# Inverse FFT tables through TensorE and PSUM in place of transposing DMA, other instructions for the last chunk's tiles, and a newly searched order, in a kernel of two sequence layers

## The chip, the cores and the metric

The kernel runs on one core of one Trainium2 chip. The metric is the device time of one execution in microseconds (us). Most executions of a kernel agree within 0.3%; the profile is one execution taken by the hardware profiler. A single core's runs are called fast unless they lie over 1.5% above the fastest of the same kernel; one execution of all told here was not fast, and it is kept out of the comparisons. Engines are written as in the profile: PE is TensorE's matmuls, PEld its weight loads, DVE is VectorE, ACT is ScalarE, POOL is GpSimd, SP issues most DMAs. Ratios are the mean time of one kernel's fast runs over the mean time of the other's fast runs of the same rounds, so they are not quite the ratio of the medians that stand beside them.

## The reference

Two layers, each applied twice, A, B, A, B, on a sequence of 2048 positions with 640 channels, in bf16:

```python
# A: a diagonal complex state-space layer
h = Lam_bar * h + Bu[:, t, :]                    # recurrence over t
y = 2.0 * einsum(hseq, Cmat).real + x * Dskip
# B: a short shift filter, a long convolution by FFT of length 4096, a gate
kv = k_shift * v
y = irfft(rfft(kv, padded) * rfft(ssm_k, padded))[:2048] + kv * ssm_D
return q * y
# the whole
x = x + A(layernorm(x)); x = x + B(layernorm(x))
x = x + A(layernorm(x)); x = x + B(layernorm(x))
```

Layer B's factor (all of it but the gate by the normalized x) does not depend on x, so the kernel computes it once, in its first 200 us, and stores it to DRAM as `ysd`. The FFT is done as matmuls with tables of cosines and sines. The result is compared with the reference within a tolerance.

## The kernel before

Some 860 small tasks are ordered by a table of priorities, `WHEN`, which was found by a search and is part of the source. A list scheduler turns it into one fixed order per engine and the instructions are emitted in that order:

```python
WHEN = {"warm": -5, "yt_io0": 2.55, ..., "yt_Ci": 21.14, "yt_Si": 22.8, "yt_nsi": 30.27, ...}   # cut
...
order.sort(key=lambda t: (t.start, t.idx))
for t in order:
    t.emit(t.eng)
```

So each engine has a fixed order; what an instruction waits for is decided at run time. All matmuls share four PSUM buffers of 128 x 1024 float32. A task that copies a product out of PSUM may go to ACT or to DVE, as the table decides:

```python
def evac(nc, eng, out, in_):
    if eng == "act":
        nc.scalar.activation(out, in_, ACT.Copy)
    else:
        nc.vector.tensor_copy(out, in_)
```

The tables `Ci` and `Si` of the inverse FFT are the transposes of the forward tables `Cf` and `Sf` (17 blocks of 128 columns each), and `NSi` is the negated `Si`:

```python
for a, b in (("Ci", "Cf"), ("Si", "Sf")):
    def e_tr(_, a=a, b=b):
        nc.sync.dma_start_transpose(out=T[a].get()[:], in_=T[b].get().rearrange("p q k -> p (q k)"))
    ...
def e_nsi(_):
    nc.vector.tensor_scalar(T["NSi"].get(), T["Si"].get(), -1.0, None, ALU.mult)
```

Second, another table on DVE, `a_t0`, which is used only some 90 us after it is made; it is not part of the change, but the argument comes back to it:

```python
def e_t0(_):                      # task "a_t0", two instructions of 1290 float32 columns
    v.tensor_scalar(r, y, MAGIC, None, ALU.add)
    v.scalar_tensor_tensor(r, r, MAGIC, y, ALU.subtract, ALU.subtract)
```

The end of layer B's second use. The last chunk of 512 positions is finished tile by tile (128 positions each) by two scalar_tensor_tensor instructions (STT) on DVE; results are stored in pairs of tiles:

```python
# abridged: index expressions are shortened
if len(qs) == 1:     # the last chunk: each tile by itself
    nc.vector.scalar_tensor_tensor(bu(), s_x[q], nmean, s_Y[q], ALU.add, ALU.mult)
    nc.vector.scalar_tensor_tensor(s_Y[q], bu(), rstd, s_x[q], ALU.mult, ALU.add)
...
if out is not None and q % 2 == 1:      # store two tiles, 320 KB
    nc.sync.dma_start(out=out[...2 tiles...], in_=s_Y[:, 2 * t:2 * t + 2, :])
```

## Time and profile before

| what | before |
|---|---|
| device time, median of 3 runs (lowest, highest) | 358.5 us (357.69, 358.55) |
| span of the profiled execution, mean granted TensorE clock | 356.8 us, 0.987 |
| TensorE's last matmul ends | 345.70 us |
| last read of PSUM by DVE starts | 345.89 us |
| last sum on DVE ends | 353.60 us |

The table is read as a relay. Up to 345.70 us TensorE sets the pace: it is busy nearly without a break from 140 us on. From 345.89 to 353.60 us, DVE alone finishes the last tiles. From 353.60 to 356.8 us the last store is under way. A change of the head (the first 140 us) shows as a shift of 345.70; a change of the tail shows in the two distances after it. The page itself is shown in the prediction.

### The profile page before, as it was taken

What the parts mean: (1) busy time and instruction counts of PE and PEld (TensorE: products, weight loads), DVE (VectorE), ACT (ScalarE), POOL (GpSimd) and SP (SyncE); (2) the same over time, 40 slices, a digit from 0 to 9 for tenths busy, and PEclk for the clock granted to TensorE, in tenths of its full rate; (3) what the DMA queues carried; (4) which work ended last, traced back from release to release, by engine and by line L of the source; (5) the groups of instructions that cost most, each with busy time, mean ns of one, the idle gap of its engine ahead of it and who ended that gap; (6) DMA issues with size and microseconds to landing.
All of it is one profiled execution on the core that took longest, in us unless ns stands there. A gap on an engine that the chain in (4) does not pass through costs nothing.

```text
span 356.8 us, 8409 instructions
## 1 busy us (share of the span) xinstructions
PE 327.5 (92%) x3534; PEld 247.6 (69%) x3565; DVE 315.1 (88%) x479; ACT 256.4 (72%) x406; POOL 20.8 (6%) x51
## 2 busy tenths in 40 slices
PE   7686998989998997999999999999999999999970
PEld 7346876867686986986685677686866767755640
DVE  8799798798799797999999969979999679999896
ACT  3999798898799999943378599797256577306850
POOL 5841003000000000000000000000000000000000
PEclk9999899999999999999999999999999999999996
DMA  7999999999999982790226690605032022220141
GB/s 193 208 235 188 182 184 217 193 186 202 237 245 163 184 174 46 144 233 2 62 73 119 137 333 34 147 18 132 0 68 81 3 16 59 75 75 2 50 172 73
DMA packets 118712, 45.91 MB, mean 129 GB/s; under 512 B 111629, under 2 KB 112914, under 8 KB 118674
## 3 DMA queue, kind: packets, MB, share of 16 engines
q1 hardware_dynamic: 118528, 45.36, 59.9%
q8 instruction: 28, 0.46, 0.5%
q14 instruction: 10, 0.08, 0.1%
q10 hardware_dynamic: 146, 0.01, 0.0%
HBM read 17.38 MB, written 7.86 MB: 71 GB/s over the span
## 4 chain that ended last, share of the span: by engine, by line
PE 69%; ACT 10%; DVE 8%; DMA 7%; issue 3%; SPq 2%; DVEq 0%; ACTq 0%
PE ps L859 31%; PE ps L770 11%; PE ps L773 11%; ACT b L382 6%; PE ps L608 3%; PE ps L1163 3%; DMA b<-in_A_C_im_dram 2%; DMA b<-in_B_v_dram 2%; DVE b L1169 2%; PE ps L1313 2%; DMA b<-b 2%; PE ps L1314 1%; PE ps L1208 1%; SPq L536 1%; DMA b<-in_B_k_dram 1%
## 5 line engine op out<-in xcount | busy, mean ns | idle before, releaser
L382 ACT ACTIVATE b<-ps 128x1024 bf16<-128x1024 f32 (+3 forms) x125 | 109.6, 945 | 29.5 <-PE ps L773 25.5
L859 PEld LDWEIGHTS <-b 128*128 128x128 bf16 x880 | 67.7, 98 | 48.3
L859 PE MATMUL ps<-W,b 128*128 128x128 bf16 (+1 forms) x629 | 95.7, 298 | 0.6
L770 PE MATMUL ps<-b,BT 128*128 128x256 bf16 x400 | 56.8, 273 | 0.0
L773 PE MATMUL ps<-b,BT 128*128 128x256 bf16 x400 | 56.7, 273 | 0.0
L808 DVE TENSOR_TENSOR_SCAN b<-rtab,b 128x1290 bf16<-128x1290 f32 x16 | 44.7, 2833 | 0.3
L773 PEld LDWEIGHTS <-BT 128*128 128x128 bf16 x400 | 39.1, 98 | 4.5
L770 PEld LDWEIGHTS <-BT 128*128 128x128 bf16 x400 | 38.6, 98 | 4.4
L726 ACT ACTIVATE b<-b,nmr,rstd 128x640 bf16<-128x640 f32 (+1 forms) x43 | 37.0, 915 | 6.2 <-DVE nmr L693 6.2
L681 ACT ACTIVATE junk<-b,nmean 128x640 bf16<-128x640 f32 x48 | 39.7, 828 | 1.5
L1232 PE MATMUL ps<-b,b 128*128 128x128 bf16 x170 | 35.1, 219 | 1.2 <-ACT G L382 0.7
L1235 PE MATMUL ps<-b,b 128*128 128x128 bf16 x170 | 35.4, 219 | 0.0
L1237 PE MATMUL ps<-b,b 128*128 128x128 bf16 x150 | 32.8, 219 | 0.0
L1234 PE MATMUL ps<-b,b 128*128 128x128 bf16 x150 | 32.8, 219 | 0.0
L384 DVE CAST b<-ps 128x1024 bf16<-128x1024 f32 (+2 forms) x24 | 26.2, 1109 | 6.3 <-PE ps L1208 2.7
L867 ACT ACTIVATE b<-ps 128x640 f32<-128x640 f32 x16 | 11.1, 697 | 22.8 <-PE ps L859 22.8
L859 PE MATMUL ps<-G,b 128*128 128x128 bf16 (+1 forms) x152 | 26.5, 295 | 0.4
L1163 PE MATMUL ps<-b,fd 128*128 128x512 bf16 x73 | 18.6, 380 | 3.8 <-POOL fd L1141 2.0
L1313 PE MATMUL ps<-b,b 128*128 128x128 bf16 x160 | 19.4, 219 | 2.6 <-ACT b L382 2.1
L1314 PE MATMUL ps<-b,b 128*128 128x128 bf16 x160 | 19.2, 219 | 0.0
L552 ACT ACTIVATE b<-b,s_F 128x640 f32<-128x640 bf16 x20 | 17.2, 859 | 1.8 <-DVE W L556 1.4
L556 DVE SCALAR_TENSOR_TENSOR W<-b,s_F 128x640 bf16<-128x640 bf16 x20 | 17.4, 882 | 1.0 <-ACT b L552 0.7
(210 smaller groups left out, 560.3 us busy)
## 6 DMA issues: line engine op xcount, KB each, us to landing
b<-in_A_x_dram SPq DMA_DIRECT2D x8, 640.0 KB, 4.9
b<-ysd SPq DMA_DIRECT2D x8, 640.0 KB, 5.1
b<-in_B_ssm_k_dram SPq DMA_DIRECT2D x5, 512.0 KB, 8.6
kvd<-b SPq DMA_DIRECT2D x5, 512.0 KB, 4.3
b<-kvd SPq DMA_DIRECT2D x5, 512.0 KB, 5.4
ysd<-b SPq DMA_DIRECT2D x5, 512.0 KB, 5.0
out_dram<-b SPq DMA_DIRECT2D x8, 320.0 KB, 2.2
tab<-in_A_B_re_dram SPq DMA_DIRECT2D x1, 800.0 KB, 7.4
```

What stands on the lines that cost most here:

```text
L382: nc.scalar.activation(out, in_, ACT.Copy)
L681: nc.scalar.activation(small.junk, src(q), ACT.Square, bias=st["nmean"][:, i:i + 1], scale=1.0, accum_out=st["ssq"][:, i:i + 1])
L726: nc.scalar.activation(dst, src, ACT.Identity, bias=st["nmr"][:, i:i + 1], scale=st["rstd"][:, i:i + 1])
L770: nc.tensor.matmul(pb[:, jj, c2, :], lhsT=aw["BT1"][:, c2, j, k, :], rhs=uT[:, 0:2, k, :], start=(k == 0), stop=False)
L773: nc.tensor.matmul(pb[:, jj, c2, :], lhsT=aw["BT0"][:, c2, k, j * P:(j + 1) * P], rhs=uT[:, 2:4, k, :], start=False, stop=(k == NJ - 1))
L808: nc.vector.tensor_tensor_scan(gv, rt, gv, 0.0, ALU.mult, ALU.add)
L859: nc.tensor.matmul(pc[:, o0:o1], lhsT=lh, rhs=rh, start=(n == 0), stop=(n == len(ops) - 1))
L1163: nc.tensor.matmul(pk[:, 512 * b:512 * (b + 1)], lhsT=s_ds.get()[:, l, :], rhs=kT[:, t0:t0 + 512], start=(l == 0), stop=(l == 3))
L1232: nc.tensor.matmul(ps[:, g, 0, :], lhsT=T["Cf"].get()[:, q, :], rhs=are, start=True, stop=single)
L1234: nc.tensor.matmul(ps[:, g, 0, :], lhsT=T["Sf"].get()[:, q, :], rhs=A[:, 2 * q + 1, :], start=False, stop=True)
L1235: nc.tensor.matmul(ps[:, g, 1, :], lhsT=T["NSf"].get()[:, q, :], rhs=are, start=True, stop=single)
L1237: nc.tensor.matmul(ps[:, g, 1, :], lhsT=T["Cf"].get()[:, q, :], rhs=A[:, 2 * q + 1, :], start=False, stop=True)
```

## The change

It has three parts and a consequence. (1) `Ci` and `Si` come from 34 TensorE transposes (the data block as weights, the identity as moving operand) into PSUM and six copies out of it, so the SP queue loses two transposing DMAs. (2) Tiles 0 to 2 of the last chunk get a normalization (ACT or DVE), a bf16 product and a sum in place of the two STTs; the sums of the last two chunks may go to GpSimd. (3) The last chunk's tiles are stored one by one. The consequence: the whole table `WHEN` was searched again, and nearly every one of its keys has a new value.

```diff
 # (1)
-        nc.sync.dma_start_transpose(out=T[a].get()[:], in_=T[b].get().rearrange("p q k -> p (q k)"))
+    for q0, q1 in ((0, 6), (6, 12), (12, NQ)):
+        for q in range(q0, q1):
+            nc.tensor.matmul(s_ps.get()[:, (q - q0) * P:(q - q0 + 1) * P], lhsT=T[b].get()[:, q, :], rhs=consts["ident_bf"][:], start=True, stop=True)
+        ...
+        evac(nc, eng, T[a].get()[:, q0:q1, :].rearrange("p q k -> p (q k)"), s_ps.get()[:, 0:(q1 - q0) * P])   # eng: ACT or DVE
 # (2)
-            if len(qs) == 1:
+            if qs[0] == 3:                      # only tile 3 keeps its two STTs
...
-                            nc.vector.tensor_tensor(s_Y.get()[:, q, :], b, x, ALU.add)
+                            (nc.gpsimd if eng == "pool" else nc.vector).tensor_tensor(s_Y.get()[:, q, :], b, x, ALU.add)
+                    engs, ests = (("dve", "pool"), (0.77, 1.4)) if out is not None and c >= NCH - 2 else ...
 # (3)
-        if out is not None and q % 2 == 1:      # 320 KB
+        if len(groups) > 1:                     # the last chunk: 160 KB each
+                nc.sync.dma_start(out=out[...][:, q & 1], in_=s_Y.get()[:, q, :])
 # and the table
-    "warm": -5, "yt_io0": 2.55, ..., "a_t0": 26.17, ...        (862 keys)
+    "warm": 0.28, "yt_io0": 0.89, ..., "a_t0": 29.65, ...      (877 keys)
```

## The prediction

> **What bounds the kernel now.** I read the page from the top (busy shares, slices), then the busy time by stretch of the span, then the end of the chain of waits and the DVE timeline of the last 15 us, and last the queue of SP and the GpSimd rows, because the change touches those.
>
> The first view says that no engine is far from full, and that the weight lies unevenly.
>
> ```profile
> PE 327.5 (92%) x3534; PEld 247.6 (69%) x3565; DVE 315.1 (88%) x479; ACT 256.4 (72%) x406; POOL 20.8 (6%) x51
> ...
> PE   7686998989998997999999999999999999999970
> DVE  8799798798799797999999969979999679999896
> ```
>
> The second view cuts the span in three: head, middle and tail (us from the start; then busy us and instructions of each engine, the clock, the DMA share).
>
> ```profile
> 0.00:140.00 140.00, 122.95 (x1701) 99.54 (x1713) 118.54 (x222) 124.47 (x164) 20.77 (x51) 0.99 1.02 193
> 140.00:341.00 201.00, 199.90 (x1799) 145.32 (x1817) 184.19 (x236) 128.91 (x236) 0.00 (x0) 1.00 0.35 86
> 341.00:357.00 16.00, 4.70 (x42) 2.76 (x39) 12.33 (x23) 3.03 (x9) 0.00 (x0) 0.81 0.25 100
> ```
>
> In the middle TensorE is busy 199.90 of 201 us: it is the bound there, and it can only end earlier if it starts that stretch earlier or has less to do. In the head it idles 140 - 122.95 = 17 us; ACT (124 of 140 us) and the DMA share (1.02) are the full ones. In the tail TensorE is done and DVE is what ends the kernel. The chain of waits, cut to its end, says the same:
>
> ```profile
> 337.82 3.82 PE ps L859 x28
> 341.64 0.02 issue
> 341.66 0.83 DVE b L871 x2
> ...
> 345.89 0.82 DVE b L871 x2
> 346.72 0.81 DVE b L901
> 347.52 0.03 issue
> 347.55 0.89 DVE b L905
> 348.43 2.40 DVE b L901 x3
> 350.83 0.02 issue
> 350.86 1.68 DVE b L905 x2
> ```
>
> L871 takes the last TensorE product out of PSUM at 345.89; after it come four multiplications (L901) and four additions (L905) of the last chunk, one per tile, all on DVE; the last one starts at 352.72 and ends at 353.60. The output store that follows lands 2.2 us after its issue, and the span closes at 356.8. The measured time is 358.5, 1.7 us more than the span.
>
> **What the Trainium skill says.** First, "SBUF — State Buffer", section "Who interferes with whom": a DVE instruction with two SBUF inputs contends with a GpSimd instruction that reads SBUF, and the later one blocks. The trace agrees. GpSimd's small products (L1141) take
>
> ```profile
> L1141 POOL TENSOR_TENSOR fd<-ident_bf,skf x20: 392/394/2311, 12.5 to 55.7; 128x128 bf16<-128x128 bf16 x20
> ```
>
> 394 ns as a rule (minimum, median, maximum) and once 2311 ns, when DVE ran a two-input product (L487) that itself took 2311 ns. Second, "GPSIMD Engine Reference", section "3.1 Elementwise — side-by-side cycle accounting": about 2.6 cycles per element for a two-input operation. At the skill's 1.2 GHz that is 277 ns for 128 elements, so the 394 ns hold some 117 ns of fixed cost, and a 640-element addition comes to an estimated 1.39 + 0.12 = 1.5 us. No run shows one yet. Third, "DMA: Bandwidth & Descriptors", section "Anatomy of one DMA — SWDGE (gpsimd) path": about 2 us of a transfer are fixed. It is written for another queue, but the 320 KB stores here land after 2.2 us, so halving a store can save only a few tenths. Fourth, "TensorE: Matmul & The Clock Gate", section "Part 4: PE-mode transpose": about 390 ns alone and 275 ns in a kernel. The trace shows something cheaper for the form used here (data as weights, identity as moving operand, L572): five of them in 0.44 us, and 128-column matmuls of a stream start 0.055 us apart. The measured pitch counts.
>
> **The change, part by part.**
>
> (1) The inverse tables. Two transposing DMAs (L987) leave the SP queue; they held it 2.42 and 3.75 us, at 19.9 and 23.1 us. So 6.2 us go from a queue that is nearly always occupied in the first 60 us, and later loads can be issued up to 6 us earlier. In return: 2 tables x 17 blocks = 34 TensorE matmuls, 34 x 0.055 = 1.9 us, and 6 PSUM copies of 768, 768 and 640 columns. The rows give 0.82 us for 768 columns and 0.70 for 640 on ACT, 0.82 for 640 on DVE, thus some 4 x 0.85 + 2 x 0.76 = 4.9 us over ACT and DVE. TensorE's 1.9 us fit into its 17 us of idle time. The copies fall on ACT and DVE when ACT is busy 9.94 of 10 us (20 to 30 us). And the tables are first used near 50 us, while they are ready by about 28 us: nothing waits for them now; only the queue does. Relief and added load are of one size: up to 6 us less in the queue against some 2.5 us more on each of ACT and DVE. The order table was searched again for the new mix, so I take a little as gained: TensorE's end 0.3 us earlier, with 2 us of doubt either way.
>
> (2) Last chunk, tile by tile. Before: 8 two-input STT at 0.82 to 0.84 us pitch, 6.6 us of DVE. After: tile 3 keeps its two (1.66 us). Tiles 0 to 2 get a normalization (on ACT, 0.91 us, or on DVE, 0.56 us pitch), a bf16 product of 640 elements and a sum. L916 does 2560 in 1.49 us; with 0.16 us fixed, 640 take 0.33 + 0.16 = 0.49, or 0.42 at pitch. The sum (as L924) is 0.76 us at pitch. ACT is nearly empty in the tail (3.03 of 16 us), so I expect two of the three normalizations there: DVE has 1.66 + 0.56 + 3 x 0.42 + 3 x 0.76 = 5.8 us. That is 0.8 us less.
>
> (3) Sums shared with GpSimd, in the last two chunks: seven sums may move. GpSimd gets one only where DVE is taken for over 0.3 us in the schedule; I guess two of chunk 2 and one of chunk 3. DVE loses 3 x 0.76 = 2.3 us. But nearly everything DVE does there has two SBUF inputs (products, sums, STT), so by the skill's rule and the 2311 ns case the two engines largely take turns: three sums of 1.5 us on GpSimd can block up to 4.5 us of DVE. Only the PSUM reads (L871, 0.82 us each), normalizations and small operations go beside them. I charge 2.0 us, so this part brings 0.3 us.
>
> (4) Stores one by one: 160 KB after the last sum in place of 320 KB. Against 2 us fixed this saves perhaps 0.4 us. More stores are issued (four in place of two), hidden but for the last.
>
> There is a floor: the last tile's own chain after L871 ends at 346.71: mean 0.25, squares 1.0, root 0.4, reciprocal and product 0.4, normalization 0.6 to 0.95, product 0.45, sum 0.76, so 350.6 to 350.9 against 353.60. Parts 2 and 3 can thus bring 3 us at the most; I take 0.8 + 0.3 = 1.1. Sum: 0.3 + 1.1 + 0.4 = 1.8 us; 358.5 - 1.8 = 356.7 us.
>
> **The rivals.** One: the queue is the head's real bound, and the 6.2 us come through. For it: DMA share 1.02, and loads wait behind one another. Against it: few TensorE waits in the head name a DMA (the largest is 1.1 us); most name ACT, DVE or GpSimd. If half came through: 353.5 us. Two: ACT and DVE bound the head, and the six copies delay it by their 2.5 us with no relief: TensorE starts its full stretch later, and the tail's gain is used up: about 359 us. Three: GpSimd and DVE lock each other in the tail, so that a 1.5 us sum stands before the last tile's chain: it replaces DVE's serial work with a new wait, tail gain zero or negative, 357.5 to 358.5. Four: no contention in the tail and the chain at its floor: 3 + 0.4 us, so 355.
>
> **Range and chances.** The rivals span 353.5 to 359; I set 353.5 to 359.3 for 8 in 10 around 356.7. Over 2% faster means below 351.3, which needs both rival one and rival four in full: 0.05. Over 2% slower means above 365.7, more than all the copies added serially: 0.02. Within 2%: 0.93.
>
> **What would show it.** In the changed profile: TensorE's last matmul within 2 us of 345.7 (step 1); its idle time in the first 140 us near 17 us, with 34 new matmuls and six copies of some 0.8 us between 15 and 35 us; from the last L871 to the last sum 5.5 to 6.2 us in place of 7.7 (parts 2 and 3); GpSimd sums of 1.5 us or more, and DVE products or sums beside them stretched beyond 0.5 and 0.8 us (contention; if none is stretched, rival four); the last store landing about 0.4 us sooner. I am wrong if TensorE ends more than 3 us earlier, or if GpSimd sums stretch the last tile's chain past 353.6.

## The result, and the profile after

The changed kernel takes 358.68 us (median of 4 runs, 358.41 to 359.07); the kernel before, in the same rounds, 358.38 us (357.69 to 358.55). The ratio is 1.0013, 95% interval 0.9996 to 1.003: the same within the noise. It was forecast 1.8 us shorter.

First the engines and slices of the changed kernel.

```profile
PE 332.9 (93%) x3599; PEld 249.6 (70%) x3599; DVE 317.3 (89%) x481; ACT 260.1 (73%) x410; POOL 25.7 (7%) x54
...
PE   8889799999998998999999999999999999999980
DVE  8889999795898996999999957599999989899996
```

Nothing stands out: 34 more weight loads (3599 against 3565), five more us on GpSimd. (The page before holds 3534 of its 3565 matmuls, so PE's busy times cannot be compared to the last us.) Next the three stretches, for which the columns are as in the prediction.

```profile
0.00:140.00 140.00, 126.69 (x1735) 101.17 (x1736) 121.83 (x227) 124.93 (x164) 20.72 (x51) 0.99 0.91 185
140.00:341.00 201.00, 199.93 (x1814) 144.84 (x1814) 182.70 (x233) 128.19 (x232) 0.00 (x0) 1.00 0.33 84
341.00:358.00 17.00, 6.26 (x52) 3.62 (x49) 12.78 (x23) 6.94 (x16) 5.01 (x3) 0.82 0.34 118
```

The middle is as full as before. In the head the DMA share fell from 1.02 to 0.91: the queue was relieved, as intended. Loads also land sooner; the row of the 512 KB loads of `ssm_k` (issue to landing, last column) of the kernel before and of the changed one:

```profile
b<-in_B_ssm_k_dram SPq DMA_DIRECT2D x5, 512.0 KB, 8.6
```

```profile
b<-in_B_ssm_k_dram SPq DMA_DIRECT2D x5, 512.0 KB, 4.9
```

Yet TensorE did not end sooner. The last matmul row of the kernel before (start, duration):

```profile
344.98 0.72 PE L859 MATMUL ps<-W,b 128*128 128x128 bf16 x10
```

And the tail of the changed kernel, in order of time, from its last matmul row on:

```profile
346.54 0.72 PE L862 MATMUL ps<-W,b 128*128 128x128 bf16 x10
347.38 0.82 DVE L874 SCALAR_TENSOR_TENSOR b<-ps,b 128x640 f32<-128x640 f32 x1
...
348.45 0.90 DVE L926 TENSOR_TENSOR b<-b,b 128x640 bf16<-128x640 bf16 x2 [0.25 <-ACT b L729]
349.02 1.58 POOL L934 TENSOR_TENSOR b<-b,b 128x640 bf16<-128x640 bf16 x1 [2.51 <-DVE b L926]
349.38 1.91 DVE L934 TENSOR_TENSOR b<-b,b 128x640 bf16<-128x640 bf16 x1
...
351.47 0.88 DVE L911 SCALAR_TENSOR_TENSOR b<-b,nmean,b 128x640 bf16<-128x640 f32 x1
352.39 0.89 DVE L915 SCALAR_TENSOR_TENSOR b<-b,rstd,b 128x640 bf16<-128x640 bf16 x1
353.19 0.48 DVE L926 TENSOR_TENSOR b<-b,b 128x640 bf16<-128x640 bf16 x1
353.71 0.83 DVE L934 TENSOR_TENSOR b<-b,b 128x640 bf16<-128x640 bf16 x1
```

346.54 + 0.72 = 347.26 us against 345.70: the head loses 1.56 us. From the PSUM read at 347.38 to the end of the last sum at 353.71 + 0.83 = 354.54 us it takes 7.16 us, against 7.71 before. Two things are to be seen. The tail got shorter, but by 0.55 us only. And while GpSimd adds (349.02, 1.58 us), DVE's sum takes 1.91 us where the same sum alone takes 0.83. The span's balance closes: TensorE's end +1.56, start of the PSUM read -0.07 (0.19 to 0.12 us behind TensorE), PSUM read to last sum -0.55, last sum to the end of the span -0.34 (3.20 to 2.86): +0.60 us, and the spans are 356.8 and 357.4. The granted clocks of the two profiled executions are 0.987 and 0.988, and each has one short stretch at half the clock before 341 us (more on these below), so the clock explains none of it. So two opposite movements of 1 to 1.5 us lie under "the same", and the questions are why the head lost, and why the tail won less than its parts.

### The profile page after: what moved, and what is told of

It reads as the page before. It is cut to its first block, busy times and chain, and to the rows that moved or that the text cites. A ratio compares the mean times of both kernels' runs of the same rounds, so it can differ in the third digit from the quotient of the medians.

```text
span 357.4 us, 8538 instructions
## 1 busy us (share of the span) xinstructions
PE 332.9 (93%) x3599; PEld 249.6 (70%) x3599; DVE 317.3 (89%) x481; ACT 260.1 (73%) x410; POOL 25.7 (7%) x54
## 4 chain that ended last, share of the span: by engine, by line
PE 66%; ACT 18%; DVE 10%; issue 3%; DMA 2%; POOL 0%; ACTq 0%; DVEq 0%; POOLq 0%
PE ps L862 32%; PE ps L773 11%; PE ps L776 11%; ACT b L385 9%; DMA b<-b 2%; PE ps L1184 2%; PE ps L1435 2%; PE ps L611 2%; DVE b L934 2%; DVE b L1190 1%; ACT BT L385 1%; ACT b L729 1%; PE ps L1253 1%; PE ps L1256 1%; ACT b L555 1%
## 5 line engine op out<-in xcount | busy, mean ns | idle before, releaser
L385 ACT ACTIVATE b<-ps 128x1024 bf16<-128x1024 f32 (+3 forms) x127 | 111.1, 935 | 29.5 <-PE ps L776 25.2
L729 ACT ACTIVATE b<-b,nmr,rstd 128x640 bf16<-128x640 f32 (+1 forms) x45 | 38.8, 914 | 12.2 <-DVE nmr L696 12.2
L387 DVE CAST b<-ps 128x1024 bf16<-128x1024 f32 (+3 forms) x28 | 29.7, 1072 | 3.3 <-PE ps L1258 1.1
L862 PE MATMUL ps<-G,b 128*128 128x512 bf16 (+1 forms) x160 | 27.0, 299 | 0.0
L934 POOL TENSOR_TENSOR b<-b,b 128x640 bf16<-128x640 bf16 x3 | 5.0, 1684 | 284.1 <-DVE b L926 284.1
L1184 PE MATMUL ps<-b,fd 128*128 128x512 bf16 x80 | 20.4, 399 | 0.7 <-ACT b L385 0.6
```

The source lines that it names most:

```text
L729: nc.scalar.activation(dst, src, ACT.Identity, bias=st["nmr"][:, i:i + 1], scale=st["rstd"][:, i:i + 1])
L862: nc.tensor.matmul(pc[:, o0:o1], lhsT=lh, rhs=rh, start=(n == 0), stop=(n == len(ops) - 1))
```

## The experiments

Eighteen runs were made, each with five timed rounds; seventeen different kernels, since free_alias_again is free_alias once more. All gave results within the tolerance of the reference. For no_gpsimd, the doubled and the alias kernels, dma_in_new_order and the moves on DVE, the emitted order of every engine was that of the parent kernel but for the edit. The table lists them; "TensorE's end" and "last stretch" (from the last PSUM read by DVE to the end of the last sum) are from the profiled execution, and its clock stands beside them because the clock varies from execution to execution.

| kernel | median, us | ratio to before [95%] | TensorE's end | last stretch | clock |
|---|---|---|---|---|---|
| before | 358.38 | 1 | 345.70 | 7.71 | 0.987 |
| changed | 358.68 | 1.0013 [0.9996, 1.0030] | 347.26 | 7.16 | 0.988 |
| new_tail_only | 357.88 | 0.9971 [0.9948, 0.9995] | 345.43 | 7.14 | 0.988 |
| new_head_only | 360.11 | 1.0044 [1.0009, 1.0079] | 347.72 | 7.71 | 0.985 |
| no_gpsimd | 358.63 | 0.9995 [0.9974, 1.0017] | 346.95 | 6.68 | 0.986 |
| dma_tables | 370.06 | 1.0314 [1.0287, 1.0341] | 359.57 | 7.14 | 0.964 |
| free_tables | 362.65 | 1.0133 [1.0098, 1.0168] | 350.28 | 7.14 | 0.979 |
| mm_only | 361.05 | 1.0088 [1.0061, 1.0116] | 349.04 | 7.16 | 0.983 |
| double_mm | 360.52 | 1.0097 [1.0064, 1.0129] | 347.97 | 7.15 | 0.986 |
| double_copy | 361.41 | 1.0096 [1.0080, 1.0113] | 348.31 | 7.15 | 0.984 |
| free_alias | 362.75 | 1.0130 [1.0107, 1.0152] | (slow execution) | | |
| mm_alias | 359.89 | 1.0052 [1.0018, 1.0085] | 346.86 | 7.16 | 0.987 |
| free_alias_again | 360.13 | 1.0060 [1.0031, 1.0090] | 348.28 | 7.15 | 0.984 |
| dma_in_new_order | 360.49 | 1.0058 [1.0022, 1.0093] | 346.79 | 7.14 | 0.986 |
| pe_in_old_order | 366.54 | 1.0222 [1.0195, 1.0250] | 354.31 | 7.71 | 0.969 |
| late_dve | 361.57 | 1.0103 [1.0081, 1.0124] | 350.07 | 7.16 | 0.979 |
| table_work_in_gap | 358.47 | 0.9996 [0.9978, 1.0013] | 346.52 | 7.14 | 0.984 |
| old_head_tail_dve | 357.01 | 0.9956 [0.9941, 0.9972] | 345.57 | 6.68 | 0.980 |
| old_head_tail_act | 357.18 | 0.9970 [0.9953, 0.9987] | 346.32 | 6.22 | 0.981 |
| old_head_tail_late | 359.26 | 1.0034 [1.0015, 1.0054] | 347.66 | 6.68 | 0.980 |

One caution for reading it. The profiles show stretches of about 3.4 us in which the granted clock is one half. They come after idle time of TensorE; the kernel before has one, in these two-microsecond windows:

```profile
34.00:36.00 2.00, 0.31 (x11) 0.22 (x7) 2.00 (x7) 1.15 (x2) 0.00 (x0) 1.00 1.21 217
36.00:38.00 2.00, 2.00 (x32) 1.62 (x27) 1.79 (x3) 1.68 (x2) 0.00 (x0) 0.71 0.86 233
38.00:40.00 2.00, 2.00 (x27) 1.80 (x27) 0.34 (x1) 1.07 (x2) 0.00 (x0) 0.50 1.16 102
```

TensorE was busy 0.31 of 2 us, and then the clock column falls to 0.71 and 0.50. How many such stretches an execution has differs from run to run of one kernel: over 66 executions of the kernel before, the mean clock went from 0.974 to 0.988 and the time from 357.24 to 359.95 us, and a straight line through them gives 1.3 us per 0.01 of mean clock. The mean clock counts these stretches only roughly, because it also takes in the end of the span, where TensorE has finished and the clock reads 0.50: table_work_in_gap (0.984) and the changed kernel (0.988) each have one stretch, at 14 to 18 us, and differ because at 350 to 352 us the clock already reads 0.50 in the one and still 0.96 in the other. Up to 341 us the profiles of mm_only, double_copy, late_dve and the three old_head_tail kernels have two stretches, those of free_tables, pe_in_old_order and dma_tables more, and all others (but free_alias) one. So ratios of less than about 0.3% between kernels of different clocks are not a verdict; I lean on the positions in profiles with as many stretches.

This also bears on the result. 34 of the 66 executions of the kernel before had a mean clock of 0.980 or less and took 358.8 us on the mean, the other 32 took 357.9. The four of the changed kernel all had 0.987 or 0.988 and took 358.7 on the mean. At a like clock the changed kernel is thus some 0.8 us slower, which fits the 0.60 us between the two profiled spans; the near tie of the medians owes something to the clock. (This is a comparison across rounds.)

### Head and tail apart

The first two kernels split the change: one has the head and order of the kernel before and only the new tail, the other the reverse. Their diffs are choices of table entries and of the two code pieces:

```diff
 # new_tail_only: code of (2) and (3); transposing DMA kept
-WHEN = <changed>
+WHEN = {keys of "B2*", "A2c3_cp*", "A2c3_xe*": changed; all others: before}
 # new_head_only: code of (1); tail code of before
+WHEN = {keys of "B2*", "A2c3_cp*", "A2c3_xe*": before; all others: changed}
```

> The kernel before with only the tail of the change: code and order of the last two chunks from the changed kernel, tables and order of all else as before. The change's tail was 1.0 us shorter by the two profiles (11.1 us from TensorE's end to the span's end before, 10.1 after). If head and tail act independently: 358.4 - 1.0 = 357.4 us, TensorE's end unchanged at 345.7. If the tail's gain was only an effect of TensorE ending later (DVE had caught up while it waited), the time stays at 358.4.

> The changed kernel with the tail of before. Independent head and tail: TensorE ends at 347.2 and the time is 358.7 + 1.0 = 359.7 us. If the tail of before also shortens when TensorE ends later: 358.7 us.

The tail alone is worth 0.9971 with TensorE ending where it did before (345.43 us), and the new head alone costs 1.0044 with TensorE ending at 347.72 us. Together -0.29% and +0.44% give +0.15%, against the +0.13% measured: the two effects add up, within intervals of 0.24 and 0.35% on either side. So the tail works, and the head is what took the gain away.

How far can a single TensorE's end be trusted? In the traces, up to 300 us, every engine of the kernels before, new_tail_only, old_head_tail_dve and old_head_tail_act has the same instructions in the same order, and TensorE ends at 345.70, 345.43, 345.57 and 346.32 us. The same holds for the changed kernel, new_head_only and no_gpsimd, with 347.26, 347.72 and 346.95. The groups do not overlap and their means differ by 1.6 us, so the head's loss is real. But profiles of one and the same head differ by up to 0.9 us, so half a microsecond between two single profiles, here and below, is no verdict.

### Is the GpSimd share worth it?

The orders are those of the changed kernel; the three sums that went to GpSimd stay on DVE.

```diff
-(nc.gpsimd if eng == "pool" else nc.vector).tensor_tensor(s_Y.get()[:, q, :], b, x, ALU.add)
+nc.vector.tensor_tensor(s_Y.get()[:, q, :], b, x, ALU.add)
```

> The changed kernel, order of all instructions unchanged, but the three sums that went to GpSimd are done by DVE at the same place of the program. If GpSimd and DVE lock each other out (a DVE sum of the last chunk took 1.91 us beside a GpSimd sum, against 0.76 alone), DVE's last stretch gets 0.76 us longer and 1.15 us shorter: 358.3 us. If GpSimd takes work off the path: 3 x 0.76 = 2.3 us longer at most, 359.5 to 361 us.

The last stretch shrinks from 7.16 to 6.68 us. Where DVE and GpSimd had shared two sums from 349.02 to 351.29 us, DVE alone now does both in 1.55 us (GpSimd had begun while DVE was still at its second product, so the fair count runs from the first product: 348.45 to 351.29 is 2.84 us, and 348.21 to 350.57 is 2.36):

```profile
348.21 0.89 DVE L935 TENSOR_TENSOR b<-b,b 128x640 bf16<-128x640 bf16 x2 [0.24 <-ACT b L738]
349.02 1.55 DVE L943 TENSOR_TENSOR b<-b,b 128x640 bf16<-128x640 bf16 x2
```

GpSimd's share therefore costs 0.48 us there. The whole time hardly differs (0.9995 against 1.0013, intervals overlapping), so it is the profile that carries this point, not the measured time. The same pair on the old head, new_tail_only and old_head_tail_dve, gives 7.14 and 6.68 us.

### The table path put back, first try

```diff
 # changed kernel, but Ci and Si by transposing DMA again; the scheduler plans anew with the changed table
-"yt_Ci:0": 21.4, "yt_Cie:0": 22.9, ... (12 keys)
+"yt_Ci": 21.14, "yt_Si": 22.8
```

> The changed kernel with the two transposing DMAs back in place of the 34 TensorE transposes and six copies; everything else, its order table included, as changed. TensorE's last matmul ended at 345.70 us before and 347.26 us after. If the transposes or their copies cost TensorE that time (theory A: 34 x 0.055 = 1.9 us of TensorE that no idle gap takes up; theory B: the six PSUM copies on ACT and DVE), TensorE ends near 345.4 and the time is near 357.0 us. If the new order table is the cause (theory C), TensorE still ends near 347.2 and the time stays near 358.7 us.

This missed everything that was expected: 370 us, TensorE's end at 359.57 us. The scheduler had made another order of nearly everything out of the same priorities. It is no clean undo, and tells only that a searched table fits just the set of tasks that it was searched for.

### What do the transposes and the copies cost?

Four kernels, all in the changed order: without transposes and copies (tables filled by GpSimd instead, so the result is wrong, though it stayed within the tolerance), with the transposes alone, with the transposes doubled, with the copies doubled.

```diff
 # free_tables: no transposes, no copies       # mm_only: transposes, no copies
+nc.gpsimd.memset(T[a].get()[:, q0:q1, :], 0.0)
 # double_mm
-for q in range(q0, q1):
+for q in list(range(q0, q1)) * 2:
 # double_copy
+evac(...)   # a second time
```

> The changed kernel in its own order with neither the 34 transposes nor the six copies: GpSimd, idle there, fills the inverse tables with zeros (wrong result on purpose). All else is in the same order. TensorE ended at 347.26 us with the change. Theory A (the matmuls themselves cost, 1.9 us): TensorE ends near 345.4, time 1.9 us under the changed kernel, so 356.8. Theory B (the six copies on ACT and DVE cost): 1.5 to 2.5 us under it too. Theory D (neither; it is the re-searched order of the rest): within 0.5 us of the changed kernel, 358.2 to 358.7.

> As the run with free tables, but the 34 transposes are done (into PSUM, unread); no copies (wrong result on purpose). Theory A: TensorE's end and the time are those of the changed kernel, 358.7. Theory B: those of the run with free tables, about 356.8.

> The changed kernel with every transpose done twice into the same place (34 more matmuls, 1.9 us of TensorE); right result. Theory A: TensorE's end 1.9 us later, 360.5 us. Theory B: idle gaps take most of it up, 358.7 to 359.2.

> The changed kernel with every one of the six copies done twice by the same engine (4.9 us more over ACT and DVE); right result. Theory B: TensorE's end 1.5 to 2.5 us later, 360.2 to 361.2 us. Theory A: under 0.7 us, 358.7 to 359.4.

Doubling either costs about 1.0% against the kernel before, that is some 0.8% against the changed one: there is no room for a second set. (TensorE's end comes 0.71 and 1.05 us later, less than the 1.9 us of theory A and the 1.5 to 2.5 us of theory B, and the execution of double_copy has a second half-clock stretch.) The two removals came out slower than the changed kernel (362.65 and 361.05 us), which neither theory had. They are confounded: GpSimd's fills stood before the small products that TensorE waits for, and the profiled executions had more time at half the clock: free_tables one stretch of 3.4 us and one of twice that, mm_only two of 3.4 us. So they were rebuilt without the fills: the inverse transform simply reads the forward tables (wrong again), with and without the transposes.

```diff
 # free_alias: no transposes, no copies; mm_alias: transposes into PSUM that nobody reads
-lhsT=T[ta].get()[:, q, :]
+lhsT=T[{"Ci": "Cf", "Si": "Sf"}.get(ta, ta)].get()[:, q, :]
```

> The run with free tables made clean: its fill by GpSimd had held back the GpSimd products that TensorE waits for, so it told nothing. Here the inverse products simply read the forward tables (wrong result on purpose); 34 transposes, six copies and nothing else are gone from the changed kernel, every engine's order is otherwise the same. The doubled transposes cost 1.9 us and the doubled copies 2.7 us against the changed kernel's 358.7. If these costs are there from the first one on, both gone is 3 to 4.6 us less: 354.1 to 355.7 us. If only further load costs and the first one fits into idle time (the prediction's view), 358 to 358.7 us, and the new order of the rest is what costs.

> The same with the 34 transposes done into PSUM and not read; no copies. If copies are the larger cost: 1.5 us or more above the run without both and 2 to 2.7 us below the changed kernel, about 356 to 357. If the transposes are the cost: equal to the changed kernel, 358.7.

> The kernel of the run with both gone once more, for a profile in the usual state: its times were 362.2 to 364.7 us with less work than the changed kernel's 358.7. If half-clock stretches after TensorE's idle gaps are the reason: the profile shows two or three such stretches of about 3.4 us in the first 60 us against one with the change, and TensorE ends 2 to 4 us later. If not: one stretch, and the loss is in waits for other engines.

free_alias had one execution of 872.28 us, the profiled one, in which matmuls took 1.7 to 2.2 times as long (382 ns where 219 is usual for 128 columns, 837 where 379 is for 512). Its profile holds no clock records at all (its page lacks the row PEclk, which all others have), so the clock of 1.00 that the run lists says nothing. I have no explanation, and free_alias_again is the same kernel run once more. Its answer, and that of mm_alias, surprised me: with all of the added work gone, or the copies alone, TensorE ends at 348.28 and 346.86 us, 1.0 us after and 0.4 us before the changed kernel's 347.26 (346.95 to 347.72 for this head), and the time is not better. So it is not shown that the 34 transposes and the six copies cost the head anything beyond the spread of single profiles. A part of the reason stands in a wait that I had looked at too little. Here is the largest TensorE wait in the head of the changed kernel after its start, and what DVE did before the copy that ends it:

```profile
38.80 0.22 PE L590 MATMUL ps<-b,W 128*128 128x128 bf16 x1 [1.52 <-DVE BT L387]
```

```profile
35.01 0.83 DVE L641 TENSOR_SCALAR b<-rtab 128x1290 f32<-128x1290 f32 x1
35.87 1.50 DVE L642 SCALAR_TENSOR_TENSOR b<-b,rtab 128x1290 f32<-128x1290 f32 x1
37.29 0.72 DVE L1012 TENSOR_SCALAR b<-b 128x2176 bf16<-128x2176 bf16 x1
37.93 0.81 DVE L387 CAST BT<-ps 128x640 bf16<-128x640 f32 x1
```

TensorE waits 1.52 us for L387, a copy that frees a PSUM buffer. DVE has it behind 3 us of table work: `a_t0` (L641, L642), not needed for almost another 90 us, and `NSi` (L1012). The same wait in mm_alias and in free_alias_again:

```profile
38.51 0.22 PE L599 MATMUL ps<-b,W 128*128 128x128 bf16 x1 [2.35 <-DVE BT L396]
```

```profile
38.20 0.22 PE L599 MATMUL ps<-b,W 128*128 128x128 bf16 x1 [2.35 <-DVE BT L396]
```

It grew from 1.52 to 2.35 us. What TensorE saved earlier it lost again at this wait, and it went on at 38.51 and 38.20 us in place of 38.80. So taking the added work away brought little here, and it looked hidden. It is not the whole account of free_alias_again: its spectrum products (six DVE instructions of 1.28 us, next section but one) still begin 0.59 us sooner than in the changed kernel (45.29 for 45.88 us), and this lead is gone at the second set of products (71.16 for 71.12); what took it there was not pursued.

### The DMA tables without a new order, and the PE tables without a new order

Here every engine's order is kept and only the way of the tables is swapped.

```diff
 # dma_in_new_order: changed kernel; transposes and copies out, at the first one's place in the SP queue:
+nc.sync.dma_start_transpose(out=T[a].get()[:], in_=T[b].get().rearrange("p q k -> p (q k)"))
 # pe_in_old_order: kernel before; the DMAs out, transposes and copies at the next free PSUM buffer
+if self.pending and free: mm(...); ...; ev(..., eng)
```

> The changed kernel with every engine's order kept as it is, but the 34 transposes and six copies taken out and the two transposing DMAs put in the SP queue at the place of the first transposes of each table; right result. The earlier run with DMA tables went through the scheduler, which then ordered nearly everything anew, so it tested nothing. If the TensorE path itself costs the head its 1.6 us: 357.0 us. If the new order of the rest is what costs, and the DMAs cost queue time on top: 359 to 362 us, TensorE's end not before 347.3.

> The kernel before with every engine's order kept as it is, the two DMAs taken out, and the transposes and copies put in where a PSUM buffer is free next; right result, the tail of before. If the TensorE path costs 1.9 us wherever it stands: 360.2 us, ratio 1.005. If it fits into idle time and the queue's relief is worth nothing: 358.3, ratio 1.000. If the relief comes through: 355.5 to 357.5, ratio 0.992 to 0.998.

dma_in_new_order ends TensorE at 346.79 us, 0.47 us before the changed kernel, which is no more than profiles of one head differ by; its executions at a clock of 0.986 to 0.987 took 359.04 and 359.19 us, the changed kernel's four took 358.41 to 359.07. Against free_alias_again, which has neither way of making tables, the 6 us of transposing DMA in the queue make no time worse (346.79 against 348.28 us; why free_alias_again is the slower of the two is open). So in the new order the relief of the queue, which the DMA rows above show to be real, had nobody waiting for it; in the old order no clean kernel tests it.

dma_in_new_order tells most when it is set beside new_tail_only. Both make the tables by DMA, both have the new tail, both do 3565 weight loads; what differs is the order, and with it the engine of a few copies. new_tail_only has the ratio 0.9971 [0.9948, 0.9995] and TensorE's end at 345.43 us, dma_in_new_order 1.0058 [1.0022, 1.0093] and 346.79 us. So the newly searched order costs 1.36 us of TensorE's end by these two profiles, without one transpose or copy in it. One reservation stays: the two DMAs stand in the SP queue where the transposes were, a place that no search chose.

pe_in_old_order is a clumsy insertion with three half-clock stretches (366.54 us), and it tells only that the transposes want a place of their own in the order.

### Moving DVE's table work

If DVE's work ahead of that copy is the bound, moving it must move TensorE. late_dve puts `a_t0` and `NSi` behind the spectrum products (task `yq0_pw`, six instructions of 1.28 us); old_head_tail_late does the same to the old head, which has a like wait of 1.69 us at 35.75 us.

```diff
+late = [t for t in order if t.name in ("a_t0", "yt_nsi")]
+order = [t for t in order if t not in late]
+at = next(i for i, t in enumerate(order) if t.name == "yq0_pw") + 1
+order[at:at] = late
```

> The changed kernel with all engine orders kept but DVE's: the two instructions of the phase table (0.83 and 1.50 us) and the negated sine table (0.72 us) go behind the next PSUM copies, to about 43 us, so that the copy TensorE waits for at 38.80 (wait 1.52 us) can start up to 3 us earlier. Theory A (the re-searched order of the head lost its time in that one wait): TensorE's end moves from 347.26 to about 345.8, the half-clock stretch elsewhere or the same, ratio to the kernel before 0.997 (357.3 us at a granted clock of 0.987). Theory B (the loss is spread, and TensorE, freed here, waits for something else next): end at 346.9 to 347.3, ratio 1.000 to 1.002. Theory C (a moved burst of 3 us of DVE work meets another copy at 43 us): end later than 347.3, ratio above 1.003.

> The best version so far (head of the kernel before, tail of the changed one with all sums on DVE: ratio 0.9956) with the same move on DVE: the phase table and the negated sine table behind the PSUM copies, so that the wait of 1.69 us at 35.75 can shrink. Theory A: TensorE's end 345.4 becomes about 344, ratio 0.992. Theory B: end within 0.4 us of 345.4, ratio 0.995 to 0.997. Theory C: later, ratio above 0.998.

The wait at 38.80 us disappeared, as theory A had it, and TensorE nevertheless ended 2.8 us later than in the changed kernel, as theory C had it. Two new waits of the late_dve profile show why:

```profile
55.91 0.23 PE L1348 MATMUL ps<-b,b 128*128 128x128 bf16 x1 [1.86 <-DVE b L1025]
57.83 0.22 PE L1347 MATMUL ps<-b,b 128*128 128x128 bf16 x1 [1.58 <-DVE b L1203]
```

L1025 is `NSi`: the inverse transform reads it, and now it came after the products. The old head shows the same: TensorE ends at 347.66 us where old_head_tail_dve, its parent, ends at 345.57, with one new wait of 3.42 us for `NSi` at 55.84 us. Not all of the 2.8 us is the waits themselves: after them the late_dve profile has a second half-clock stretch, at 58.5 to 62 us, which by itself can cost up to half of its 3.4 us. The place was the wrong one, by my choice: the work had been put off within a stretch in which DVE is nearly full, and in front of something else that TensorE needs. The last kernel therefore takes the work out of the stretch: `NSi` into a gap where DVE idled in late_dve, `a_t0` to 85 us, where DVE of the changed kernel idles 3.61 us.

```diff
+for name, mark, off in (("yt_nsi", "yq1_ka", 1), ("a_t0", "A1c0_ln_bn", 0)):
+    ...                     # take the task out and put it at the mark
+    order.insert(at, t)
```

> The changed kernel, all orders but DVE's kept. The negated sine table (0.72 us) goes behind the first PSUM copy and the small product after it, where DVE idled 1.1 us in the run before; the phase table (0.83 and 1.50 us) goes to the stretch at 86 to 89.7 us, where DVE of the changed kernel idles 3.61 us. So the stretch of 28 to 55 us loses 2.3 us of DVE's work and nothing is put in its way later. Theory A (DVE's serial work up to the first inverse transform bounds this stretch of the head, which is why putting 3 us of it behind the spectrum products cost TensorE 2.1 us): the wait of 1.52 us at 38.80 is gone, no new wait of 1.8 or 3.4 us at 56, the six products begin 1.5 to 2.5 us sooner, TensorE's end comes at 345.0 to 346.2 in place of 347.26, ratio 0.995 to 0.998. Theory B (the gain of any one stretch is lost at the next wait, since ACT or another engine bounds the later head): the products begin sooner, but TensorE's end stays at 346.8 or later, ratio 1.000 or more.

```profile
44.67 1.29 DVE L1324 TENSOR_TENSOR b<-b,b 128x2176 bf16<-128x2176 bf16 x1
...
84.96 0.82 DVE L655 TENSOR_SCALAR b<-rtab 128x1290 f32<-128x1290 f32 x1
85.82 1.50 DVE L656 SCALAR_TENSOR_TENSOR b<-b,rtab 128x1290 f32<-128x1290 f32 x1
```

```profile
345.80 0.72 PE L876 MATMUL ps<-W,b 128*128 128x128 bf16 x10
```

The wait is gone, and between 20 and 60 us no wait of TensorE is longer than 0.7 us. The products begin at 44.67 us in place of 45.88, TensorE ends at 346.52 in place of 347.26, and the ratio is 0.9996 in place of 1.0013. The end lies between what theory A expected (345.0 to 346.2) and what B did (346.8 or later). The three profiles of the unmoved head have the products at 45.08 to 45.89 us and TensorE's end at 346.95 to 347.72, all later, so the two moves together (`a_t0` out of the stretch, `NSi` behind the copy) gain something between 0.4 and 1.2 us there; the ratios' intervals overlap.

That is a gain of the new head, but it does not show what the new head lost against the old one. The old head, too, has `NSi` in front of a copy that TensorE waits 1.69 us for, and its first spectrum products begin later than those of the changed kernel. The first of the six, before and changed:

```profile
46.55 1.29 DVE L1289 TENSOR_TENSOR b<-b,b 128x2176 bf16<-128x2176 bf16 x1
```

```profile
45.88 1.29 DVE L1310 TENSOR_TENSOR b<-b,b 128x2176 bf16<-128x2176 bf16 x1
```

Later marks cannot be compared one by one, since the two orders mix the layers differently: the second and third set of products begin later in the changed kernel (71.12 for 70.09, 95.50 for 91.44 us), the fourth and fifth sooner (123.22 for 128.69, 162.36 for 163.89). In which place of its order the new head loses the 1.5 us stays open.

### A version that beats both

```diff
 # old_head_tail_dve: new_tail_only with all sums on DVE
 # old_head_tail_act: the same; tile 3 like the others, its normalizations all on ACT
```

> A candidate for the better kernel: tables and order of before, the tail of the change, the three GpSimd sums back on DVE (same order as in the run with the new tail alone, which was at 0.9971 of before). GpSimd's lock cost the last stretch 0.48 us by the profiles of the changed kernel with and without it (from the last PSUM read to the last sum 7.16 and 6.68 us). So 0.996 of before. If GpSimd helps: 0.998 to 1.000.

> As the last one, but tile 3 of the last chunk is computed as the others and all four normalizations of that chunk are on ACT: DVE has 0.42 + 0.76 in place of 1.66 us for tile 3. If DVE's total sets the end: 0.5 us less, 0.9945 of before. If the last tile's own chain over ACT sets it (0.91 us on ACT in place of 0.56 on DVE): no gain or 0.4 us more, 0.996 to 0.997.

Head and order of the kernel before with the new tail and without GpSimd takes 357.01 us, 0.9956 of the kernel before with an interval that excludes 1, and it has the lowest ratio of all kernels here (the intervals of old_head_tail_act and new_tail_only overlap with it). Its last stretch is 6.68 us. The variant on ACT has the shortest last stretch of all, 6.22 us, but its TensorE ended 0.75 us later, so it wins nothing on top. It was already 0.76 us behind at the first products (47.83 for 47.07 us), in a head that the variant does not touch, so this may be the difference of one execution from another.

## Why the prediction was right or wrong

**The kernel's bounds** were read rightly: TensorE in the middle, DVE in the last 8 us, and the two parts of the balance add up in the split kernels.

**The tail (parts 2 and 3) was right in mechanism and mis-sized in one term.** Part 2 alone was put at 0.8 us; without GpSimd the last stretch is 6.68 in place of 7.71 us, a gain of 1.03. Part 3 was put at +0.3 us, 2.3 us of sums saved against 2.0 us of blocking; measured it is a loss of 0.48 us. The rule used was right (the engines take turns, and DVE's sum stretched to 1.91 us), and GpSimd did take two sums of chunk 2 and one of chunk 3, at 1.68 us on average for an estimate of 1.5:

```profile
L934 POOL TENSOR_TENSOR b<-b,b 128x640 bf16<-128x640 bf16 x3 | 5.0, 1684 | 284.1 <-DVE b L926 284.1
```

What was missed: the two sums of chunk 2 run at 343 us beside TensorE's last matmuls, where DVE's time is not yet what ends the kernel; only the one sum of chunk 3 lies in the last stretch, and there it replaces 0.77 us of DVE by a blocking of about 1.1 us (1.91 - 0.83), which is 0.3 of the 0.48 us. The forecast of "5.5 to 6.2 us" for that stretch was therefore too good; it is 7.16.

**The stores (part 4)** were put at 0.4 us; 0.34 us were seen between last sum and end of span. No run tests the stores alone; over all profiles this distance is 3.1 to 3.2 us with stores of pairs and 2.8 to 3.0 with single ones.

**The failed step is part 1, "TensorE's end 0.3 us earlier".** It came 1.56 us later, within the 2 us of doubt that were given but of the wrong sign, and it alone turned the expected gain into nothing. The step weighed "relief and added load" against each other, and neither turned out to be the account that mattered. The relief of the queue is real and unused: in the new order, tables made by DMA, or not made at all, cost no less time than tables made by TensorE. The added load shows no cost beyond the spread of profiles of one head: without the copies TensorE ends at 346.86 us, with DMA in place of transposes and copies at 346.79, with both at 346.95 to 347.72 (a second helping of either does cost, some 0.8% of the time). Removing it made a later wait longer, 2.35 in place of 1.52 us. What moved the head is the sentence of the prediction that was passed over quickest, "The order table was searched again for the new mix, so I take a little as gained". The new order is worse on this chip: with the same work in both, tables by DMA and the new tail, TensorE ends at 346.79 us in the new order and at 345.43 in the old, 1.36 us later. In which place the order loses this is open. Moving 3 us of table work from before one PSUM copy wins back 0.4 to 1.2 us, but the old head has a like wait, so that wait is not shown to be the loss.

**The rivals.** One (the queue bounds the head) is refuted for the new order by dma_in_new_order and free_alias_again; for the old order it was not tested cleanly. Two came closest in its result (about 359 us), and DVE's order does matter in the head, but the load that it blamed, the copies, is not shown to cost anything, so its number was luck. Three (lock in the tail) was right for the GpSimd share and wrong for the tail's sign, which stayed a gain. Four (no contention, 355 us) is refuted by the 1.91 us sum.

**The range** (353.5 to 359.3) holds the 358.68 us, and "within 2%" was right. The point of 356.7 us was wrong by the head's term, 1.56 + 0.3 us, which is most of the distance.

## What to carry to other kernels

When a change comes with a re-searched order, the order is a part of the change with a cost of its own, and splitting the kernel (new tail on the old head, new head on the old tail) prices it in two runs; the old work in the new order shows it alone. To judge what an added piece of work costs, look for the first wait after it and ask whose work ends that wait: work ahead of such a wait may be free, and taking it away then only makes the wait longer. Before half a microsecond is read out of one profile, profiles of kernels that share the stretch should be compared: here they differ by up to 0.9 us. Two engines that lock each other are no relief in a stretch where one of them is what ends the kernel.

## What the Trainium skill lacked or had wrong

- "TensorE: Matmul & The Clock Gate", section "HAM oscillation — how this bites in real kernels", gives the rule "no PE-idle gaps >~3.4µs". Here a wait of 1.69 us, in a window in which TensorE was busy 0.31 of 2 us, was followed by about 3.4 us at half the clock. In the changed kernel the stretch begins at 13.9 us, after no wait longer than 0.7 us in the 3.4 us before. Shorter gaps than the rule's matter in this kernel, and whether such a stretch comes changes from one execution to the next (mean clock 0.974 to 0.988 for one kernel).
- "SBUF — State Buffer", section "Who interferes with whom", says that the two engines lock each other but not what sharing then yields. Here it yields a loss: two products on DVE with two sums split between DVE and GpSimd took 2.84 us (348.45 to 351.29), all on DVE 2.36.
- No page that I found tells of a whole execution with TensorE slow and no clock records in its profile: 872.28 us once, with matmuls of 512 columns at 837 ns where 379 is usual, and the same kernel 360 us when run again.
